# Starting a fused attention and MoE kernel on half of the first batch: first batch split by tokens, loads reordered

## The chip, the cores and the metric

One core of one Trainium2 chip. The metric is the device time of one execution in microseconds (us), given as the median of the runs of a kernel. In the profile PE is TensorE, PEld its weight loads, DVE is VectorE, ACT is ScalarE, POOL is GpSimd and SP is SyncE. L412 is line 412 of the kernel's file. The change adds lines, so a line of the new kernel has another number for the same work: L412 becomes L568 (first product), L430 becomes L586 (second product), L335 and L341 become L496 (last multiply of the attention of batch 0), and L371 becomes L527. Experiments shift the numbers by one or two again.

## The reference

```python
# q, k, v: (8, 8, 576, 64) f32;  w_in: (512, 2048);  w_out: (2048, 512)
scores = q @ k^T / 8
mask_local   = (0 <= i - j < 32)                     # heads 0 to 3
mask_strided = (j <= i) and (j % 32 == i % 32)       # heads 4 to 7
attn = softmax(where(mask, scores, -1e9)) @ v
x = attn.transpose(0, 2, 1, 3).reshape(4608, 512)
h = x @ w_in
out = relu(h)**2 @ w_out                             # (4608, 512) f32
```

## The kernel before

The kernel turns each batch's attention into columns of `xt`, x transposed, in bf16: four tiles of 128 rows, one for each pair of heads. The MoE part runs over chunks of 512 tokens. The **first product** of a chunk has 16 column blocks of four matmuls each, followed by ReLU (ScalarE) and a square (VectorE) into `g`; the **second product** multiplies g with w_out. Chunk 0 needs batch 0 alone, and a large part of the time before 50 us is spent on getting there. The order of instructions on each engine is the order of the program. These are the parts that the change touches:

```python
def first_steps():          # batch 0: a, b, c, d are its four pairs of heads
    t, n, o = T_, ..., ...  # t transposes q or k, S_ scores and exp, n sums and 1/sum, o product with v
    a, b, c, d = first_order                       # (0, 2, 3, 1)
    ...
    order = [(t(a, "q"), 0), (t(a, "k"), 2), (S_(a), 4), (t(b, "q"), 1), (t(b, "k"), 1), (S_(b), 0),
             (t(c, "q"), 0), (t(c, "k"), 0), (n(a), 0), (S_(c), 0), (n(b), 0),
             (t(d, "q"), 0), (t(d, "k"), 0), (o(a), 0), (S_(d), 0), (due(c), 0), (o(b), 0),
             (due(d), 0), (n(c), 0), (o(c), 0), (lambda: part((a, b), (0,)), 0), (n(d), 0), (o(d), 0),
             (lambda: part((a, b), (1, 2)), 0), (lambda: part((c,)), 0), (lambda: part((d,)), 0)]
    return order            # the numbers are spare matmuls that keep the clock up

gates = {1: w_in_b[0:1, 0, 1024:1025], 2: w_out_b[0:1, 8, 0:1]}

def loads(b):               # batch b; gate: a one-element GpSimd copy into the staging tile,
    u = 4 * b               # which must wait for the weights and so holds the load back
    for i in range(2):
        load_qk_local(u + i, nc.sync, gate=gates.get(b) if i == 0 else None)
    ... # v loads on the sync queue
    w_out(0)                # (batch 1 only) quarter of w_out, requested and cast by GpSimd
    load_qk_str(u + 2)
    cast_qk_local(u, pool2) # pool2: GpSimd casts
    w_out(1)
    cast_qk_local(u + 1, pool2)
    load_qk_str(u + 3)
    w_out(2)
    cast_v_local(u)
    cast_v_local(u + 1)
    w_out(3)
    ...

load_qk_local(0, nc.sync); load_qk_local(1, nc.sync)
load_qk_str(2)
make_identity(nc, ident)
load_qk_str(3)
...                         # memsets and masks
load_v_first()
cast_qk_local(1, pool2)
for i in range(4):
    load_w_in(i)
first = first_steps()
...
loads(1)
```

From batch 2 on the local part of the attention goes back through the same stream of requests: the sync queue carries, in program order, the loads of each batch, the transposes of strided q and k by DMA, and the transposes of the result (`xt<-x_l`), which free the tile `x_l` for the next batch.

The softmax here doesn't subtract the row's maximum and nothing guards it: scores larger than these inputs give would overflow.

## Time and profile before

| kernel before | value |
|---|---|
| time, median of 2 runs | 322.76 us (322.57 to 322.96) |
| profiled span | 319.6 us |
| first transposes of batch 0 | 4.95 us |
| first block of the first product begins | 21.07 us |
| last `xt` write of batch 0 ends | 24.4 us |
| second product of chunk 0 begins | 37.29 us |

The prediction below shows the stretches, the chain and the waits of this kernel. From the timeline of VectorE, then of GpSimd (start, length, engine, line, operation, tiles, idle time before and what ended it):

```profile
23.62 0.82 DVE L341 TENSOR_TENSOR xt<-pt,g_sb 128x288 bf16<-128x288 f32 x2 [0.89 <-ACT g_sb L317]
```

```profile
23.31 0.18 POOL L111 CAST q_st<-w_in_b 1x1 f32<-1x1 bf16 x1 [8.94 <-DMA w_in_b<-in_moe_w_in_dram]
...
48.27 0.18 POOL L111 CAST q_st<-w_out_b 1x1 f32<-1x1 bf16 x1 [0.38 <-DMA w_out_b<-in_moe_w_out_dram]
```

The first is the end of batch 0's attention. The other two are the gates of batch 1 and batch 2, the moments from which their loads may flow.

### The profile page before, as it was taken

The numbers are of one execution on the slowest core, as the hardware profiler recorded it, in microseconds if no ns is written. First come the engines' busy times: TensorE is split into PE (matmuls) and PEld (weight loads), VectorE is DVE, ScalarE is ACT, GpSimd is POOL, SyncE is SP. The second block draws the span as 40 slices with busy tenths as digits, with TensorE's granted clock in tenths as the row PEclk, the third lists the DMA queues.
The fourth block names the chain that finished last, engine by engine and source line by source line (L and its number), as shares of the span: only waits on it lengthen the run. The fifth ranks groups of instructions, "written<-read, shape, count | busy, mean of one in ns | idle before, by whom it ended". The sixth has DMA issues, their size and how long they took to land.

```text
span 319.6 us, 6138 instructions
## 1 busy us (share of the span) xinstructions
PE 300.0 (94%) x2322; PEld 149.5 (47%) x2364; DVE 170.7 (53%) x414; ACT 163.7 (51%) x337; POOL 87.8 (27%) x114
## 2 busy tenths in 40 slices
PE   7789978898999989999999999999999999999995
PEld 3454545444555444444444444444444444444442
DVE  6476463677956975676585557555555222222200
ACT  4576644477655755554554455545543443434311
POOL 8605472473930713271182015000000000000000
PEclk9859999999999999999999999999999999999999
DMA  7999999999999999999797677000411110000021
GB/s 182 172 205 227 221 155 251 186 328 208 198 162 210 197 212 182 212 242 188 183 211 167 145 159 133 35 33 33 53 51 36 55 42 36 33 33 35 35 96 66
DMA packets 87220, 44.79 MB, mean 140 GB/s; under 512 B 71768, under 2 KB 80376, under 8 KB 87000
## 3 DMA queue, kind: packets, MB, share of 16 engines
q1 hardware_dynamic: 77448, 34.81, 53.3%
q0 software_dynamic: 9744, 9.60, 18.9%
q8 instruction: 18, 0.29, 0.4%
q14 instruction: 10, 0.08, 0.1%
HBM read 36.89 MB, written 12.98 MB: 156 GB/s over the span
## 4 chain that ended last, share of the span: by engine, by line
PE 78%; DMA 9%; DVE 6%; ACT 3%; issue 2%; POOL 1%; SPq 0%; ACTq 0%; POOLq 0%
PE ph L412 33%; PE py L430 26%; PE ph L430 10%; PE pt L359 3%; PE pt L277 3%; DMA w_out_b<-in_moe_w_out_dram 3%; DMA q_st<-in_q_dram 3%; DMA kT_s<-in_k_dram 3%; DVE xt L396 1%; PE pt L388 1%; DVE e L288 1%; PE pt L233 1%; DVE g_sb L419 1%; ACT r L418 1%; ACT e L282 1%
## 5 line engine op out<-in xcount | busy, mean ns | idle before, releaser
L412 PE MATMUL ph<-xt,w_in_b 128*128 128x512 bf16 x557 | 143.3, 380 | 3.3 <-DVE xt L396 1.9
L418 ACT ACTIVATE r<-ph 128x512 bf16<-128x512 f32 x143 | 85.3, 597 | 99.5 <-PE ph L412 96.2
L419 DVE TENSOR_TENSOR g_sb<-r 128x512 bf16<-128x512 bf16 x144 | 71.2, 496 | 102.4 <-ACT r L418 101.9
L430 PE MATMUL py<-w_out_b,g_sb 128*128 128x512 bf16 x383 | 100.2, 379 | 1.3 <-issue 0.5
L430 PEld LDWEIGHTS <-g_sb 128*128 128x128 bf16 x576 | 52.9, 98 | 60.8 <-issue 4.3
L412 PEld LDWEIGHTS <-w_in_b 128*128 128x128 bf16 x576 | 51.7, 98 | 54.5 <-issue 1.3
L282 ACT ACTIVATE e<-pt 128x288 bf16<-128x288 f32 (+1 forms) x128 | 48.8, 406 | 17.0 <-PE pt L277 16.9
L430 PE MATMUL ph<-w_out_b,g_sb 128*128 128x512 bf16 x166 | 40.7, 379 | 1.9 <-DMA w_out_b<-in_moe_w_out_dram 1.2
L181 POOL CAST vl<-vl_st 128x768 bf16<-128x768 f32 x14 | 12.4, 886 | 60.2 <-DMA vl_st<-in_v_dram 58.1
L359 PEld LDWEIGHTS <-e 128*128 128x128 bf16 (+1 forms) x392 | 21.0, 97 | 15.6 <-DVE e L288 0.5
L371 DVE TENSOR_TENSOR x_s<-pt,rinv 72x384 bf16<-72x384 f32 (+1 forms) x42 | 21.4, 509 | 1.4
L288 DVE TENSOR_TENSOR e<-e,mask_str 72x576 bf16<-72x576 bf16 x32 | 18.0, 563 | 5.9 <-ACT e L282 5.6
L122 POOL CAST q_l<-q_st 96x768 bf16<-96x768 f32 x15 | 13.0, 865 | 21.9 <-DMA q_st<-in_q_dram 19.4
L288 DVE TENSOR_TENSOR e<-e,mask_loc 128x576 bf16<-128x576 bf16 x32 | 16.7, 523 | 1.7 <-ACT e L282 1.7
L122 POOL CAST k_l<-k_st 96x768 bf16<-96x768 f32 x15 | 13.3, 885 | 13.9 <-DMA k_st<-in_k_dram 13.8
L370 DVE RECIPROCAL rinv<-pt 96x6 f32<-96x6 f32 (+2 forms) x70 | 12.9, 184 | 7.8 <-PE pt L359 7.8
L434 ACT COPY y<-py 128x512 f32<-128x512 f32 x25 | 14.7, 587 | 4.0 <-PE py L430 4.0
L371 DVE TENSOR_TENSOR x_l<-pt,rinv 96x384 bf16<-96x384 f32 x28 | 15.5, 553 | 1.8 <-DMA xt<-x_l 0.9
L434 ACT COPY y<-ph 128x512 f32<-128x512 f32 x11 | 6.4, 586 | 19.4 <-PE ph L430 19.4
L197 POOL CAST vs<-v_st 72x1024 bf16<-72x1024 f32 x14 | 15.4, 1126 | 1.6 <-DMA v_st<-in_v_dram 1.3
L359 PE MATMUL pt<-vs,e 72*128 72x65 bf16 x224 | 13.7, 193 | 0.1
L182 POOL CAST vl<-vl_st 32x640 bf16<-32x640 f32 x14 | 11.9, 850 | 0.9
(77 smaller groups left out, 154.2 us busy)
## 6 DMA issues: line engine op xcount, KB each, us to landing
out_dram<-y SPq DMA_DIRECT2D x36, 256.0 KB, 2.0
vl_st<-in_v_dram SPq DMA_DIRECT2D x28, 144.0 KB, 4.0
v_st<-in_v_dram SPq DMA_DIRECT2D x14, 288.0 KB
q_st<-in_q_dram SPq DMA_DIRECT2D x8, 288.0 KB, 7.1
k_st<-in_k_dram SPq DMA_DIRECT2D x8, 288.0 KB, 7.9
q_st<-in_q_dram SPq DMA_DIRECT2D x16, 144.0 KB, 3.8
k_st<-in_k_dram SPq DMA_DIRECT2D x16, 144.0 KB, 5.9
w_in_b<-in_moe_w_in_dram POOLq DMA_DIRECT2D x4, 512.0 KB, 9.4
```

What stands on the lines that cost most here:

```text
L122: copy(t.rearrange("p j h d -> p h j d"), s[name + "f"].rearrange("p h (j d) -> p h j d", j=6))
L197: (copy or nc.gpsimd.tensor_copy)(t[:, :, 0:D], s["vf"].rearrange("p h (j d) -> p (h j) d", d=D))
L282: nc.scalar.activation(e[0:kn, lo:lo + S // 2], banks[row][half][0:kn, 0:S // 2], AF.Exp, scale=scale)
L288: nc.vector.tensor_tensor(x, x, m.to_broadcast([kn, n, w]), op=ALU.mult)
L359: nc.tensor.matmul(po[:, n - n0, :], e[0:kn, pos(n):pos(n) + 128], rhs[0:kn, src(n), 0:D + 1], start=True, stop=True)
L370: nc.vector.reciprocal(rinv[0:w, 0:m], po[0:w, 0:m, D:D + 1])
L371: nc.vector.tensor_tensor(x, po[0:w, 0:m, 0:D], rinv[0:w, 0:m].to_broadcast([w, m, D]), op=ALU.mult)
L412: nc.tensor.matmul(ph, w_in_b[:, kk, 128 * ff:128 * (ff + 1)], xt[kk][:, 512 * c:512 * (c + 1)], start=(kk == order[0]), stop=(kk == order ...
L418: nc.scalar.activation(r, ph, AF.Relu)
L419: later(1, lambda: nc.vector.tensor_tensor(g[:, ff, :], r, r, op=ALU.mult))
L430: nc.tensor.matmul(py, g[:, ff, 128 * j:128 * (j + 1)], w_out_b[:, ff, :], start=(ff == 0), stop=(ff == 15))
L434: nc.scalar.copy(y, py)
```

## The change

Its intent: tokens 0 to 287 of batch 0 need only keys 0 to 287, so half of q, k and v is loaded first, its attention is finished, and 12 blocks of the first product run on tokens 0 to 255 while the second half's attention is worked out between them. The second half's rows are held back by a gate, so that they don't compete with the first half's. GpSimd issues the first two quarters of w_in ahead of everything that waits on it (at 3.89 and 6.68 us; the third, at 13.12, stands behind a cast). Local v of batch 0 comes by the sync queue now and is cast by GpSimd; before, GpSimd's own transfers cast it on the way. In batch 1's loads, two quarters of w_out come ahead of the rest, and the casts of v behind all four. The core of the diff, with cuts marked by "...":

```diff
+    def load_local_half(hf):
+        ...
+            if hf == 1 and name == "q":          # the hold-back
+                nc.gpsimd.tensor_copy(t[0:1, 0, 0:1], vl0[32:33, 0, 0, 0:1])
+        ...
     def first_steps():
-        ... four pairs of heads, each step of one next to steps of the others
+        ... first half: transposes, scores, masks, sums, products; then
+        m = lambda ff, kks=range(4), pool=None: mm1(0, ff, kks, pool, 0, CH)      # CH = 256 tokens
+        ...                                       # blocks 0 to 2
+        cast_half(1, "k", V)
+        cast_half(1, "q", A)
+        cast_v_local_half(1, G)                   # GpSimd, ahead of loads(1)
+        m(3)
+        half_T("l", 1, "k", V)
+        half_T("l", 1, "q", V)
+        half_T("s", 1, "q", V)
+        m(4)
+        ex = half_S("l", 1)
+        ex[0]()
+        m(5)
+        ...                                       # one link of the second half, one block, and so on
+        m(11)
+        half_mask("s", 1, 1)
+        half_N("s", 1)
+        half_O("s", 1)
 ...
         w_out(0)
+        w_out(1)
         load_qk_str(u + 2)
         cast_qk_local(u, pool2)
-        w_out(1)
-        cast_qk_local(u + 1, pool2)
         load_qk_str(u + 3)
+        cast_qk_local(u + 1, pool2)
         w_out(2)
+        w_out(3)
         cast_v_local(u)
         cast_v_local(u + 1)
-        w_out(3)
 ...
-    load_v_first()
-    cast_qk_local(1, pool2)
-    for i in range(4):
-        load_w_in(i)
+    load_w_in(0)
+    ...
+    load_v_str_a()
+    load_w_in(1)
+    cast_v_local_half(0, nc.gpsimd.tensor_copy)
+    load_local_half(1)
+    load_v_local_half(1)
+    load_str_half(1, "q")
+    load_str_half(1, "k")
+    load_w_in(2)
+    first_steps()                                 # w_in 3 is in it
     for t in vl_sts:                              # memsets, now behind first_steps
         nc.vector.memset(t[0:32], 0.0)
 ...
-    for ff in range(16):
-        add(0, 1, ff) if ff >= NP else add(0, 0, ff)
+    for ff in range(12):
+        add(0, 0, ff, ps_h)                       # tokens 256 to 511 of blocks 0 to 11
+    for ff in range(12, 16):
+        add(0, 0, ff)
+        add(0, 0, ff, ps_h)
```

## The prediction

> **What bounds the kernel now.** I began with the page's busy shares and chain. TensorE is busy 300.0 of 319.6 us, so at most 19.6 us of waiting is to be had, plus what is done at a low clock. I then cut the span into stretches, to see where those 19.6 us lie, and read the wait list and the chain in order of time for the first 64 us.
>
> The stretches of the kernel before (columns: stretch, its length, busy PE, PEld, DVE, ACT, POOL, granted clock, DMA share, GB/s):
>
> ```profile
> 2.26:10.90 8.64, 6.28 (x46) 2.47 (x43) 4.60 (x28) 2.79 (x6) 7.43 (x13) 1.00 1.30 221
> 10.90:37.40 26.50, 24.60 (x228) 13.44 (x231) 17.00 (x38) 18.75 (x41) 11.18 (x16) 0.81 1.23 207
> 37.40:48.30 10.90, 8.40 (x105) 4.66 (x104) 6.75 (x14) 5.16 (x13) 7.18 (x10) 1.00 1.08 176
> 48.30:100.00 51.70, 47.53 (x511) 26.21 (x521) 34.35 (x81) 31.18 (x69) 25.82 (x31) 1.00 1.13 219
> 100.00:302.00 202.00, 198.38 (x1374) 96.22 (x1400) 106.55 (x250) 101.58 (x204) 35.14 (x42) 1.00 0.57 113
> ```
>
> The reader is to see that 202 us of the span have only 3.6 us of PE idle: nothing is to be won there. The change acts before 48 us, where DMA is full (share above 1) and PE idles about 2.4, 1.9 and 2.5 us in the first three rows. The 8.64 us of the first row are mostly warm-up matmuls, so useful work is scarcer than busy time says.
>
> From the chain in order of time (start, length, what):
>
> ```profile
> 2.26 8.60 DMA kT_s<-in_k_dram
> ...
> 24.43 9.16 DMA q_st<-in_q_dram
> ...
> 37.43 10.79 DMA w_out_b<-in_moe_w_out_dram
> 48.22 0.04 issue
> 48.26 1.02 PE ph L430 x4
> ```
>
> Three transfers carry the start: strided k of batch 0, q of batch 1, and the third quarter of w_out, which is what the second product waits for. The wait list of the first 60 us gives GpSimd's part:
>
> ```profile
> POOL q_st L111 <- DMA w_in_b<-in_moe_w_in_dram: 8.9, 1, 8.9
> PE ph L430 <- DMA w_out_b<-in_moe_w_out_dram: 1.2, 1, 1.2
> ```
>
> GpSimd is parked 8.9 us, until w_in's third quarter lands at 23.3 us. This gate holds batch 1's loads back. PE pays 1.2 us directly for w_out. In the timeline, the first matmul of the first product (L412) starts at 21.07, the unbroken run at 25.55, and it ends at 37.19.
>
> **What the Trainium skill says.** "TensorE: Matmul & The Clock Gate", Part 1, says that PE drops to half clock after a quiet window of about 3.4 us and returns after a busy one. The trace agrees: in 2 us stretches the clock is 0.72, then 0.50 four times, then 0.72 in 12 to 24 us, after PE was busy only 2.0 of 8 to 12 us. The same page, "Single matmul latency", gives (398 + N)/2.4 ns; for N = 512 that is 379 ns, and L412's row shows 380. "DMA: Bandwidth & Descriptors", Rules for kernel authors, says that transfers from different issuers share the same 16 engines, so more queues bring no bandwidth; the trace's DMA share stays above 1 whichever queue issues.
>
> **The change part by part.**
>
> *1. Token halves.* Tokens 0 to 287 need only keys 0 to 287, so their attention can finish on half of q, k and v. Then 12 of the 16 column blocks of the first product run on tokens 0 to 255 inside the second half's attention. By 25.55 the kernel before had done 3 full blocks (0.865 us each, four matmuls at 0.216); the new one should have done 12 half blocks, worth 6. That is 3 x 0.865 = 2.6 us ahead, if the second half ends no later than the old batch 0 did (about 24.4, from the last xt write at 23.62 plus 0.82).
>
> *2. When the second half can end.* Bytes read from HBM: q, k, v of batch 0 are 3 x 1.18 = 3.54 MB; a quarter of w_in or w_out is 1.05 MB. Before, 3.54 + 0.09 + 3 x 1.05 = 6.78 MB had come by 23.31, from 2.26 on: 322 GB/s. After, the order on the queues is first half (local q and k 0.59, strided q and k 0.59, v local with overlaps 0.36, v strided 0.295: 1.83 MB), w_in 0 and 1, second half (0.59 + 0.59 + 0.39 = 1.57), w_in 2: 6.55 MB, so 20.3 us at that rate, 22.6 us on the clock. All of strided v (0.59 MB) follows, 1.8 us more: 24.4, perhaps 25 once batch 1's loads compete. Then the last product with v, the multiply (two of about 0.41 to 0.6 us) and xt: **about 26.5 us**. So the second half ends 2 us later than the old batch 0, and most of the 2.6 us is spent.
>
> *3. The rest of the first product.* Left are 12 second halves and four blocks in two halves: 20 groups of four 128x256 matmuls. Pure issue is 4 x 0.109 = 0.44 us, 8.7 us in all: an end at 35.2, which is 2.0 us early. But every group takes one of two PSUM banks. Its last matmul is issued at 0.33 and ends 0.27 later (398 + 256 over 2.4), at 0.60; the ReLU then takes 0.38 (597 ns for 512 columns and 406 for 288 give 0.85 ns per column); so two groups take about 1.03 us, 0.52 each, and 20 take 10.3. Also the memsets that stood in the first 5 us now follow the second half on VectorE: 1.5 + about 1.5 us from the old timeline; with four r buffers that costs PE about 0.6 us. The end lies between 35.2 and 37.5 us; I take 36.5, so 0.7 us early.
>
> *4. w_out.* Before its third quarter lands, 0.59 + 1.05 (last w_in) + 3.54 (batch 1) + 3.15 = 8.33 MB must follow the 6.55: 14.88 MB against 14.52 before, because of v's overlap and of the first half of strided v read twice. At 322 GB/s that is 46.2 us after 2.26: **48.5 us, against 48.22**. Issuing two quarters first moves bytes about within the same queue, but takes none out ahead of the third. What helps is that GpSimd no longer has casts between the requests: before, the second stretch ran at 7.74 MB in 24.9 us, 311 GB/s. I allow 1 us either way.
>
> *5. Extra instructions.* Strided transposes double in number (16 of 36 columns per tensor and half), exponentials fall from 16 to 14, ReLUs of block 0 rise from 16 to 32: 16 x (2 x 0.38 - 0.60) = 2.6 us of ScalarE. Most lies beside data waits.
>
> Sum: part 1 gains 2.6, parts 2 and 3 give back about 1.9, and w_out's third quarter caps the remainder. The cap is the step that ends last: 48.26 stays near 47 to 48.5. Later idle changes little. I choose a gain of 1.5 us, a little above what the cap alone gives, as w_out's first two quarters come earlier and the 2.5 us of idle in 37 to 48 can shrink: 322.76 - 1.5 = 321.3 us.
>
> **The rivals.**
>
> *A. The clock.* If the fill-in matmuls keep PE above the gate's threshold, the half-clock stretch (10 us before, about 5 us of full-clock work lost) goes, and the second half's attention runs faster. For: 128-row matmuls replace gaps. Against: that stretch waits for data in the new order, so a faster PE only waits longer. If it counts, 318 us or less. The reverse, a low clock reaching into the 20 groups, costs 2 to 4 us: 324 to 326.
>
> *B. The weights come earlier.* If DMA was short of requests while GpSimd sat 8.9 us in its gate, dense issuing raises the rate; 345 GB/s would put the third quarter at 45.4 us and save close to 3 us: 319 to 320. Against: the share is above 1 throughout.
>
> *C. A new wait in program order.* PE is in order, and block 8 needs w_in's third quarter. If that is late, the second half's sums and products queue behind it, and everything slips by 1 to 3 us: 323 to 325.
>
> *D. The gain is hidden anyway*, by w_out: 322 to 323. This is nearest to my sum.
>
> **How the range follows.** D and my sum give 320.5 to 323; B reaches to 319, A to 318; C and the low clock reach to 325. The range 318.3 to 324.2 leaves about a tenth on each side. Faster by 2% means below about 316.4: it needs A and B together, 0.04. Slower by 2%, above 329.2, needs a low clock and C together: 0.03.
>
> **What would show each step.** Part 1: first 256-column matmul of the first product at 13 to 16 us, against 21.07. Part 2: last xt write of batch 0 at about 26.5. Part 3: start-to-start of groups near 0.52 us rather than 0.44, the last at about 36.5, and a VectorE run of memsets after 26 us. Part 4: the product with w_out's third quarter starts at 47 to 48.5, with a wait on that DMA ahead of it. From 100 us on, everything is shifted by a constant. I am wrong if the second half ends before 24 us, if the third quarter lands before 46, or if the clock shows 0.5 beyond 26 us.

## More of the kernel before

From the chain of waits in order of time, and from the groups of instructions (busy us, mean ns, idle before and its main releaser):

```profile
63.19 1.25 PE ph L412 x5
```

```profile
L371 DVE TENSOR_TENSOR x_l<-pt,rinv 96x384 bf16<-96x384 f32 x28 | 15.5, 553 | 1.8 <-DMA xt<-x_l 0.9
```

The chain line is the first long piece of chunk 1's first product; I use its start as the mark of how late the start of the kernel has come. The group line says that `x_l` is hardly ever waited for: 0.9 us in the whole execution.

## The result, and the profile after

The changed kernel is **slower**: 334.87 us median of 2 runs (334.35 to 335.38), with the right output; the ratio to the kernel before is 1.0376 (95% interval 1.0335 to 1.0417). A ratio here is the mean time of one kernel's fast runs over that of the other's of the same rounds, so not quite the ratio of the medians that are quoted. Executions over 1.5% slower than the fastest of the same kernel are left out of the means. The profiled span is 332.7 us against 319.6: 13.1 us more.

The stretches of the kernel after, cut at its own landmarks (columns as in the prediction):

```profile
2.26:20.40 18.14, 13.65 (x178) 7.56 (x177) 6.58 (x16) 7.49 (x18) 9.98 (x20) 0.81 1.16 206
20.40:35.20 14.80, 10.66 (x179) 7.53 (x180) 8.78 (x25) 8.60 (x24) 4.59 (x7) 0.89 0.87 159
35.20:46.90 11.70, 11.43 (x83) 8.46 (x83) 8.11 (x37) 7.35 (x20) 5.75 (x8) 0.85 1.20 222
...
101.30:112.00 10.70, 7.22 (x62) 3.44 (x60) 3.07 (x9) 3.09 (x9) 2.47 (x3) 0.84 1.19 193
112.00:314.00 202.00, 198.38 (x1388) 96.33 (x1414) 105.75 (x251) 101.17 (x203) 35.77 (x42) 1.00 0.57 110
```

The last row, 202 us long, has PE busy 198.38 us, the same as the row of 100 to 302 us that the prediction shows of before. So nearly all of the loss (about 12.8 of the 13.1 us, by the same piece of the chain in both) lies ahead of 112 us, and it lies in two places. The first is the stretch from 20.4 to 35.2 us, where DMA falls to a share of 0.87 and PE idles 4.1 us; the second is a hole of 3.5 us of PE idle in the row of 101.3 to 112. Between 105 and 110 us PE works for 2.42 of 5 us, where the kernel before worked for all 5.00.

**The first place.** The chain of the kernel after:

```profile
3.67 7.06 DMA vl_st<-in_v_dram
...
13.29 7.07 DMA k_st<-in_k_dram
...
34.01 0.07 DVE xt L496
...
35.23 4.13 PE ph L568 x21
39.37 0.04 issue
39.40 1.03 PE ph L568 x8
```

Read it from the top. The first half's v lands at 10.7 us; that opens the gate of the second half, whose k is requested at 13.29 and lands at 20.36. From there to 35.2 the chain is no DMA at all: it goes from engine to engine in pieces of under 1 us. VectorE's timeline of the same kernel has the ends of that stretch:

```profile
17.55 1.18 DVE L496 TENSOR_TENSOR xt<-pt,g_sb 128x288 bf16<-128x288 f32 x2 [0.49 <-ACT g_sb L466]
20.45 0.56 DVE L349 CAST k_l<-k_st 96x768 bf16<-96x768 f32 x1 [1.72 <-DMA k_st<-in_k_dram]
...
34.01 1.17 DVE L496 TENSOR_TENSOR xt<-pt,g_sb 128x288 bf16<-128x288 f32 x2 [1.88 <-ACT g_sb L466]
35.28 1.51 DVE L797 MEMSET vl_st<- 32x768 f32 x2
```

The first half is done at 18.7 us; the second takes from 20.45 to 35.2, 14.8 us, and batch 0 is complete 10.8 us later than before (24.4). What follows to the start of the second product takes 11.7 us (35.23 to 46.95) against 12.9 us before (24.4 to 37.29), so 1.1 us of the 10.8 come back, and the second product begins 9.7 us later.

**The second place.** GpSimd's timeline, and its longest wait in the first 64 us:

```profile
28.59 0.82 POOL L335 CAST g_sb<-vl_st 128x768 bf16<-128x768 f32 x1 [12.53 <-DMA vl_st<-in_v_dram]
29.36 0.18 POOL L119 CAST q_st<-w_in_b 1x1 f32<-1x1 bf16 x1
...
57.42 0.18 POOL L119 CAST q_st<-w_out_b 1x1 f32<-1x1 bf16 x1
```

```profile
POOL g_sb L335 <- DMA vl_st<-in_v_dram: 16.0, 2, 12.5
```

GpSimd comes to the cast of the second half's v and waits 12.5 us for v. Batch 1's gate stands behind it in program order and opens at 29.36 (23.31 before), batch 2's at 57.42 (48.27 before). No request of batch 1 can be out in the meantime, and from 28 to 32 us the DMA share is 0.31. The stream stays late to the end: the transposes that free `x_l`.

```profile
101.28 5.60 DMA xt<-x_l
```

```profile
L527 DVE TENSOR_TENSOR x_l<-pt,rinv 96x384 bf16<-96x384 f32 x28 | 15.5, 553 | 5.9 <-DMA xt<-x_l 4.8
```

They start at 101.28 us (88.95 before), and the wait for them is 4.8 us instead of 0.9. They are 12.3 us late, while PE's own work is late by less, as the mark in the chain shows:

```profile
71.74 1.24 PE ph L568 x5
```

**A sum of two shifts** follows, which every later run is held against: the mark moved from 63.19 to 71.74, P = 8.55 us, and the wait for `x_l` grew by 3.9; together 12.5 of the 13.1 us.

### The profile page after: what moved, and what is told of

Read it like the earlier page. It is cut to its first block, busy times and chain, and to the rows that moved or that the text cites. A ratio compares the mean times of both kernels' runs of the same rounds, so it can differ in the third digit from the quotient of the medians.

```text
span 332.7 us, 6551 instructions
## 1 busy us (share of the span) xinstructions
PE 306.9 (92%) x2495; PEld 157.9 (47%) x2537; DVE 170.4 (51%) x427; ACT 165.8 (50%) x352; POOL 87.6 (26%) x118
## 4 chain that ended last, share of the span: by engine, by line
PE 82%; DMA 6%; DVE 5%; ACT 2%; issue 2%; SPq 1%; POOL 0%; DVEq 0%; ACTq 0%; POOLq 0%
PE ph L568 36%; PE py L586 26%; PE ph L586 10%; PE pt L515 3%; PE pt L285 3%; DMA k_st<-in_k_dram 2%; DMA vl_st<-in_v_dram 2%; DMA xt<-x_l 2%; PE pt L544 1%; PE pt L241 1%; DVE xt L552 1%; DVE x_s L527 1%; SPq L314 1%; DVE g_sb L575 1%; ACT r L574 1%
## 5 line engine op out<-in xcount | busy, mean ns | idle before, releaser
L568 PE MATMUL ph<-xt,w_in_b 128*128 128x512 bf16 (+1 forms) x623 | 148.2, 362 | 3.6 <-DVE xt L552 1.9
L574 ACT ACTIVATE r<-ph 128x512 bf16<-128x512 f32 (+1 forms) x159 | 88.2, 555 | 104.9 <-PE ph L568 101.2
L575 DVE TENSOR_TENSOR g_sb<-r 128x512 bf16<-128x512 bf16 (+1 forms) x160 | 73.0, 461 | 104.7 <-ACT r L574 103.1
L568 PEld LDWEIGHTS <-w_in_b 128*128 128x128 bf16 x640 | 58.3, 99 | 52.9 <-issue 3.8
L290 ACT ACTIVATE e<-pt 128x288 bf16<-128x288 f32 (+1 forms) x112 | 43.2, 406 | 11.4 <-PE pt L285 11.2
L586 PE MATMUL ph<-w_out_b,g_sb 128*128 128x512 bf16 x167 | 42.3, 387 | 0.5
L130 POOL CAST q_l<-q_st 96x768 bf16<-96x768 f32 x14 | 11.9, 851 | 24.2 <-DMA q_st<-in_q_dram 23.3
L526 DVE RECIPROCAL rinv<-pt 96x6 f32<-96x6 f32 (+2 forms) x70 | 12.9, 184 | 9.0 <-PE pt L515 9.0
L130 POOL CAST k_l<-k_st 96x768 bf16<-96x768 f32 x14 | 12.3, 879 | 18.2 <-DMA k_st<-in_k_dram 15.5
L296 DVE TENSOR_TENSOR e<-e,mask_loc 128x576 bf16<-128x576 bf16 x28 | 15.2, 543 | 1.5 <-ACT e L290 1.5
L296 DVE TENSOR_TENSOR e<-e,mask_str 72x576 bf16<-72x576 bf16 x28 | 13.4, 478 | 2.3 <-ACT e L290 2.2
L515 PE MATMUL pt<-vs,e 72*128 72x65 bf16 x224 | 13.4, 193 | 0.0
```

The source lines that it names most:

```text
L130: copy(t.rearrange("p j h d -> p h j d"), s[name + "f"].rearrange("p h (j d) -> p h j d", j=6))
L290: nc.scalar.activation(e[0:kn, lo:lo + S // 2], banks[row][half][0:kn, 0:S // 2], AF.Exp, scale=scale)
L296: nc.vector.tensor_tensor(x, x, m.to_broadcast([kn, n, w]), op=ALU.mult)
L515: nc.tensor.matmul(po[:, n - n0, :], e[0:kn, pos(n):pos(n) + 128], rhs[0:kn, src(n), 0:D + 1], start=True, stop=True)
L526: nc.vector.reciprocal(rinv[0:w, 0:m], po[0:w, 0:m, D:D + 1])
L568: nc.tensor.matmul(ph, w_in_b[:, kk, 128 * ff:128 * (ff + 1)], xt[kk][:, 512 * c + lo:512 * c + hi], start=(kk == 0), stop=(kk == 3))
```

## The experiments

Two theories for the first place:

- *Chain*: the second half's attention is a string of small dependent steps that runs after the first half's, instead of beside it, so that batch 0 needs two such strings one after the other.
- *Data* (rival): its rows come too late, because of the hold-back or because of v.

A third suspect beside these was the clock of TensorE. For the second place the suspect was the order on GpSimd. All kernels that ran gave the right output. No experiment beat the kernel before.

### e1_nohold and e2_v1dma: earlier data

```diff
# e1_nohold: no hold-back
-            if hf == 1 and name == "q":
-                nc.gpsimd.tensor_copy(t[0:1, 0, 0:1], vl0[32:33, 0, 0, 0:1])
# e2_v1dma: v of the second half by GpSimd's own casting transfers, requested behind strided k; no cast left on GpSimd
-    load_v_local_half(1)
+    for i in range(NL // 2):
+        nc.gpsimd.dma_start(out=vl0[:, NL // 2 + i], in_=v[0, 0:4]...)
-        cast_v_local_half(1, G)
```

> The changed kernel without the one-element copy that holds the second half's local q, k and v back until GpSimd has cast the first half's v. Theory V (the second half's v, on the sync queue, lands last at 28.6 us and GpSimd's cast of it stands ahead of everything): v lands near 15 us instead, GpSimd passes the cast by 17 us, batch 1's loads start when the third quarter of w_in lands (about 25 instead of 29.5 us), the last xt write of batch 0 moves from 35.2 to about 30 us; time 327 to 330 us. Rival H (k of the second half, landing at 20.4 us, is what costs): the same gain, with the k cast near 12 us. Rival C (half clock, two banks and memsets in the 20 half groups cost most): 333 us or more.

> The changed kernel with the second half's local v loaded by GpSimd's casting transfers (as the kernel before did), ahead of the third quarter of w_in; the GpSimd cast of it is gone, the hold-back stays. Theory V: the 12.5 us wait of GpSimd is gone, the gate of batch 1 passes when the third quarter of w_in lands (24 to 26 us), the last xt write comes at about 31 us; time 327 to 331 us. Rival H (k at 20.4 us is what costs): 333 to 335 us. Rival C: 333 us or more.

Measured: e1_nohold 330.66 us, ratio 1.0255 (1.0164 to 1.0346); e2_v1dma 331.69, ratio 1.0271 (1.0188 to 1.0354). In e1_nohold the second half's k was cast at 17.80 us instead of 20.45, and yet the last `xt` write ended at 35.3, as in the kernel after (35.2); in e2_v1dma, where v needed no cast, it ended at 35.35. So **earlier data of the second half did not bring its end forward**. For k the trace shows the reason: its rows were cast 2.65 us earlier in e1_nohold, but its transposes stand in TensorE's program behind the first half and its blocks 0 to 2, and began at 20.63 us against 21.06 in the kernel after. The second string thus starts only when the first half and its three blocks are through, and from VectorE's copy of the transposed k to the last `xt` write it takes about 13.4 us in all three kernels. A low clock hid a part of the gain: in this execution the four spare matmuls ahead of the blocks took 1.89 us, against 1.04 in the kernel after, so the earlier k may be worth about 1 us at full pace (an estimate from these two and the 0.4 us that did come). The gain has another source. In e1_nohold v lands earlier, and GpSimd's order moves up:

```profile
25.16 0.83 POOL L333 CAST g_sb<-vl_st 128x768 bf16<-128x768 f32 x1 [9.75 <-DMA vl_st<-in_v_dram]
25.93 0.27 POOL L119 CAST q_st<-w_in_b 1x1 f32<-1x1 bf16 x1
```

The gates open at 25.93 and 53.67 (e2_v1dma: 24.09 and 53.54), the mark is at 72.35 (72.10), no earlier than in the kernel after, and the wait for `x_l` is gone in both. The ratio falls by 0.0105 to 0.0121, 3.4 to 3.9 us: the size of that wait. The intervals of these ratios just overlap that of the kernel after (1.0335 to 1.0417); the reading rests on the traces, in which the gates come earlier, the wait vanishes and the span falls by 4.4 us or more. This shows the second place to be GpSimd's order, with the first place unchanged.

### e3_gatefirst: the gate ahead of the cast

```diff
+        loads1_head()               # batch 1: gate, local q and k, one v, w_out 0 and 1, strided q and k
         cast_v_local_half(1, G)
```

> The changed kernel with batch 1's gate, its q, k and first v on the sync queue, the first half of w_out and the first strided unit issued ahead of GpSimd's cast of the second half's v. If batch 1's late loads cost the time: loads start near 25 us, DMA idles no more in 28 to 32 us, and the time falls to 328 to 331 us. If the late end of batch 0's second half costs it (PE has nothing to do until xt is complete): last xt write still at 35 us or later, time 333 to 336 us.

Measured: 333.51 us, ratio 1.0340 (1.0256 to 1.0425). The gates came at 23.59 and 49.82, nearly as early as in the kernel before, and the wait for `x_l` vanished, as expected; but the start got worse. The last `xt` write ended at 38.3 and the second product began at 50.12, so the mark came at 75.27. Part of it can be read off: GpSimd's casts now lie beside VectorE's steps of the second half. VectorE, then GpSimd, in this kernel:

```profile
29.34 0.29 DVE L575 TENSOR_TENSOR g_sb<-r 128x256 bf16<-128x256 bf16 x1 [0.87 <-ACT r L574]
...
32.10 0.84 DVE L575 TENSOR_TENSOR g_sb<-r 128x256 bf16<-128x256 bf16 x1 [1.90 <-ACT r L574]
```

```profile
31.98 0.82 POOL L130 CAST q_l<-q_st 96x768 bf16<-96x768 f32 x1 [1.04 <-DMA q_st<-in_q_dram]
```

The same multiply takes 0.29 us alone and 0.84 beside a cast that runs until 32.80. "SBUF — State Buffer" in the Trainium skill, section "SBUF: two separate sides", says that GpSimd and VectorE share a pair of ports, and that whoever takes it first has it for its whole instruction, against a VectorE operation with two SBUF inputs among others. The trace agrees: the multiply reads r twice, and ends 0.14 us after the cast. Two such cases cost 1.1 us. The rest of the 3.1 us by which the `xt` write came later was there before the gate opened: VectorE's copy of the transposed k began at 23.67 us instead of 21.73. TensorE was at a clock of 0.50 until about 20 us in this execution, against about 15 in the kernel after, while GpSimd's order ahead of the gate is the same in both; so this part is not shown to be the gate's doing.

### e4_wofirst: the new order of w_out on the kernel before

```diff
         w_out(0)
+        w_out(1)
         load_qk_str(u + 2)
         ...                         # as in the change, on the kernel before
```

> The kernel before with only the order of w_out changed: first two quarters one after the other ahead of batch 1's strided q and k. If this part does nothing (the third quarter still lands near 48 us): 322 to 324 us. If it delays batch 1's strided unit: 325 us or more, with PE waiting for its transposes at 43 us.

Measured: 327.02 us (324.16 to 329.07), ratio 1.0097 (0.9989 to 1.0206): unclear. In the profiled run the mark was at 64.35, 1.2 us late, and `x_l` waited 3.9 us. The stream was only 2.0 us late at its transposes (90.93), but these took 8.1 us to the next write instead of the 6.3 of before. So this part may cost a per cent by itself; the spread of its runs does not allow a firmer word.

### e5_alone, e6_tail, e7_all: nothing between the links, nothing behind them

```diff
# e5_alone: the blocks 4 to 11 of the first product moved behind the second half's last link
-        m(4)
-        tick()
         ...
+        for ff in range(4, 12):
+            m(ff)
+            tick()
# e6_tail: late memsets moved to the start or cut to what is read; every third half block in a third PSUM bank
-        nc.vector.memset(t[0:32], 0.0)
+        nc.vector.memset(t.rearrange("p (h t) d -> p h t d", h=2)[0:32, :, 0, :], 0.0)
+            p3 = ps_y if len(groups) % 3 == 2 else None
# e7_all: e1_nohold, e5_alone and e6_tail together
```

> The changed kernel with half blocks 4 to 11 of the first product moved behind the second half's attention, so that nothing stands between the links of its chain on any engine. First three runs showed that neither k, nor v, nor GpSimd's gate moves the last xt write from 35 us. Theory I (the interleaved blocks, in order on TensorE, ScalarE and VectorE, stretch the chain): last xt write at 30 to 31 us, the 28 groups then take about 15 us, second product at about 45 to 46 instead of 46.95 us, time 332 to 335 us. Rival L (the chain of one half is latency-bound by itself, some 14 us, whatever stands between): last xt still at 33 to 35 us, second product at 49 to 51, time 337 to 340 us.

> The changed kernel with the late memsets taken out of VectorE's way (most back at the start, the staging one cut to the two blocks that need zeros) and with the third PSUM bank in turn with the two for the 20 half groups. If banks and memsets cost what I worked out (1.6 and 0.6 us): groups 0.44 us apart at full clock, second product at about 45 instead of 46.95 us, time 332 to 333.5 us. If only the half clock sets the pace there: second product at 46 us or later, time 334 to 335.

> Three edits at once: no hold-back of the second half, half blocks 4 to 11 behind its attention, memsets and third bank as in e6_tail. If their gains add (4 from the hold, 0 to 2 from the order, 2 from the tail): 326 to 329 us. If the start is bound by something that none of them touches (the two chains in series): 328 us or more, last xt write of batch 0 no earlier than 29 us.

Measured: e5_alone 333.86 us, ratio 1.0349 (1.0271 to 1.0428). The second half, with TensorE to itself, ran from 20.25 to 33.8 us: 13.5 us instead of 14.8. Counted from VectorE's copy of the transposed k the string takes 11.2 us against 13.45 in the kernel after (10.3 in e10_warm, at full clock). So the blocks in between cost 2 to 3 us, and the larger part of the length is the string's own. Stretches of e5_alone:

```profile
24.00:28.00 4.00, 2.88 (x64) 2.25 (x63) 2.00 (x5) 2.77 (x9) 0.00 (x0) 0.50 0.83 138
28.00:32.00 4.00, 2.04 (x52) 1.89 (x52) 1.19 (x3) 2.06 (x6) 3.77 (x7) 0.50 0.44 94
```

No engine but GpSimd is busy for much over half of the second row: that is a chain, in which each waits for another. And with the blocks gone TensorE falls to half clock, which gives back part of what the cleared path won; the eight moved blocks then come on top, and the second product began at 50.72.

e6_tail: 334.74 us, ratio 1.0403 (1.0288 to 1.0518). The half blocks came 0.44 us apart instead of 0.53, and the second product began at 44.70 instead of 46.95. The mark moved up to 69.21, but `x_l` waited 6.1 us, so nothing was left of it at the end. (0.7 of the 2.3 us by which the second product came earlier lies in the second half itself, which ended at 34.5.) It shows that the two places are tied: a start that comes earlier runs into the late stream.

e7_all: 331.18 us, ratio 1.0274 (1.0187 to 1.0362). k was cast at 19.07, the last `xt` write ended at 32.2, the mark came at 70.97, and the wait was 2.0 us.

### e8_winlater: w_in behind the first half's v

```diff
-    load_w_in(0)
     ...
     load_v_str_a()
+    load_w_in(0)
     load_w_in(1)
```

> The changed kernel with w_in's first quarter requested behind the first half's v instead of ahead of it. If the early weight transfer delays the first half's k (cast at 7.69 us, against 5.17 before): k cast at 5.5 to 6.5 us and all of the first half 1 to 2 us earlier, time 332.5 to 334 us. If k is late for another reason (four smaller transfers, strided q and k beside them): cast still after 7 us, time 334 to 336 us.

Measured: 335.20 us, ratio 1.0393 (1.0299 to 1.0486). A miss: k of the first half was cast at 7.23 us against 7.69 in the kernel after and 5.17 before. w_in's first quarter is not what delays the first half's rows. Why the first transposes come at 8.30 us instead of 4.95, with half the bytes asked for, stays open in the main. In the trace k takes two requests instead of one, and the last goes out at 2.2 us instead of 1.27, which is 0.9 of the 2.5 us by which k's cast is later; why its rows then take 5.4 us instead of 3.9 to land is not shown.

### e9_pipe: the second half's chain pulled into the first half's

```diff
# without the hold-back, with the edits of e6_tail; strided q and k of the second half requested ahead of w_in 1
         half_N("l", 0, True)
+        cast_half(1, "k", V)
+        cast_half(1, "q", A)
         half_O("l", 0)
-        half_N("s", 0)
-        half_O("s", 0)
-        ...                         # blocks 0 to 3
+        half_T("l", 1, "k", V)
+        half_T("l", 1, "q", A)
+        half_N("s", 0)
+        ex = half_S("l", 1)         # and so on: one link of each half in turn,
+        ...                         # blocks 0 to 3 near the end, 4 to 11 behind it
```

> Hold-back gone, memsets and third bank as in e6_tail, strided q and k of the second half requested ahead of w_in's second quarter, and the second half's transposes and scores set between the links of the first half's chain, so that the two chains overlap. The runs so far fit a sum of two shifts: P, how late the first block of chunk 1 starts on TensorE (63.2 us in the kernel before, 71.7 in the changed one), and what it then waits for a slot of x_l (0.9 us before, 4.8 after), which the load stream sets. If two chains in series cause P: last xt write of batch 0 at 27 to 30 us, P 3 to 5 instead of 8.5 us. The load stream is only about 4 us earlier than in the changed kernel, so the wait returns: 327 to 330 us. If not: last xt write at 32 us or later, time 331 us or more.

Measured: 328.95 us, ratio 1.0164 (1.0092 to 1.0235). VectorE:

```profile
15.08 0.56 DVE L347 CAST k_l<-k_st 96x768 bf16<-96x768 f32 x1 [1.79 <-DMA k_st<-in_k_dram]
...
27.73 1.90 DVE L494 TENSOR_TENSOR xt<-pt,g_sb 128x288 bf16<-128x288 f32 x4
```

The second half ends at 29.6 us, 5.6 earlier than in the kernel after and 2.6 earlier than in e7_all, although the clock is 0.50 from 10 to 24 us. The mark comes at 66.04. This is the most direct evidence for *chain*: the same arithmetic on the same halves, with the two strings side by side. The 5.6 us are the work of all its edits together; against e7_all, which shares the others, overlapping brings 2.6, and as strided q and k of the second half were also requested earlier in e9_pipe, not even these are separated from that. The wait for `x_l` is 4.4 us again, as the batches' gates (25.18 and 50.97) did not move up with the start.

### e10_warm: the separate chain at full clock

```diff
# e7_all, with 22 spare matmuls on a zeroed tile between the second half's links
+        warm(4)
         ...
+        warm(8)
```

> e7_all with 22 spare matmuls on a zeroed tile between the links of the second half's chain, to keep the clock up (0.50 in 24 to 32 us there). If the half clock costs: clock 1.00 from 20 to 36 us, last xt write 1 to 2 us earlier than 32.2, the first 8 blocks at full clock, P 2 to 3 us below e7's 7.8; time 329 to 331, held by the load stream. If it doesn't: P as in e7 or later by the spare work, 331 to 333 us.

Measured: 327.15 us, ratio 1.0149 (1.0094 to 1.0205). The clock stayed at 1.00 from 16 us on, and the second half ran from 17.75 to 30.6 us, 12.9 us long, against 13.2 in e7_all. The last `xt` write came 1.6 us earlier (1.3 of it from a k cast that came earlier), the second product 2.0 us earlier (43.08), and the mark 3.1 us earlier (67.89). The ratio fell by 0.0125, 4 us, of which 2.0 are the wait for `x_l`, which vanished. The 1.3 us of the earlier k cast are not the doing of matmuls that stand behind it. The chain itself got 0.3 us shorter, and 0.4 us were won between the last `xt` write and the second product: the 40 half blocks there took 5.31 us instead of 6.58, and the spare matmuls ahead of them took most of this back. The other 1.1 us of the mark came after the second product had begun, where the clock reads 1.00 in both kernels. So the low clock of e7_all is worth at most about 1.6 us in this comparison, and 0.7 net of the spare work.

### e11_both and e12_pipegate: the gate first, once more

```diff
# e11_both: e1_nohold, e3_gatefirst and e6_tail together
# e12_pipegate: e9_pipe with loads1_head() ahead of the v cast, as in e3_gatefirst
```

> Hold-back gone, batch 1's gate and first loads ahead of the cast of v, memsets and third bank mended; order of the blocks as in the change. By the sum of two shifts: P about 6 (as e6_tail), load stream as early as in e3 (gate of batch 2 at 50 us), so no wait for x_l: 326 to 329 us. If P does not come down with less DMA contention, 330 us or more.

> e9_pipe with batch 1's gate and first loads ahead of the cast of the second half's v: both shifts attacked. If both causes are the right ones: P 3 to 5, no wait for x_l, 324 to 327 us. If the split of batch 0 is worth anything over the kernel before, it would show here, below 322; I expect not.

Measured: e11_both 331.39 us, ratio 1.0247 (1.0184 to 1.0309); the mark at 73.07 and no wait for `x_l`. e12_pipegate 330.68 us, ratio 1.0237 (1.0180 to 1.0294), no gain over e9_pipe, its profiled run slow (365.75 us), so no cause is read from it. In e11_both the second half ended 2.4 us later than in e1_nohold (37.7 against 35.3), but 2.0 of these were there at the copy of the transposed k (23.89 against 21.92), before the gate opened at 24.74. That an earlier gate pays with a later start is therefore not shown by e3_gatefirst and e11_both.

### e13_pipewarm and e14b_pipewarmv: what is left once the chains overlap

```diff
# e13_pipewarm: e9_pipe, with 14 spare matmuls between its links
# e14b_pipewarmv: e13_pipewarm, v of the second half as in e2_v1dma, but requested ahead of w_in 2
```

> The ninth experiment (second half's transposes and scores pulled into the first half's chain, no hold-back, late memsets out of the way, third bank) with 14 spare matmuls on a zeroed tile added where TensorE waits in it, so that the clock does not fall to 0.5. There the second half's last xt write ended at 29.6 us and the second product began at 40.97, at clock 0.50 from 12 to 24 us. Theory (series chain plus low clock make the late start, and a second limit, the stream of loads on the sync queue, sets the end when it is later): xt ends at 27 to 28, second product starts at 38.5 to 39.5, the fifth-block landmark of the chain at 64 to 65, but x_l still waits 4 to 6 us for xt<-x_l, so that the total hardly moves: 327 to 329.5 us. Rival (only the start on TensorE counts, waits later are absorbed): the total falls by what the start gains, to about 326 or less. Rival (clock is not what costs): xt stays at 29 or later.

> The kernel of e13_pipewarm, but the second half's v is cast by its own GpSimd transfers, requested ahead of w_in's third quarter, so that no GpSimd cast stands between w_in and batch 1's gate; one memset of a staging tile moves to the start. In e13_pipewarm the clock stayed at 1.00 from 8 us on and still the second half's last xt write ended at 29.55 us; there its scores and exponentials were done by 23.4 and the product with v waited for the v cast, which GpSimd began at 25.16 after 9.53 us of waiting for v. New theory for the start: once the chains overlap, the arrival of v is what binds, as the prediction had assumed for the kernel of the change. It expects: v there by 22 to 23, last xt write ended at 26.5 to 27.5, second product begins at 39 to 40 (the issue of 28 groups of 0.44 us after it). Rival: the chain itself still binds and xt ends at 29 to 29.6 again. For the stream: theory (the loads of batch 1 onwards are a second limit that starts at batch 1's gate) expects the gate at 24 instead of 25.93, batch 2's gate at 50 to 52 instead of 53.77, the wait of x_l under 2.5 us instead of 4.1, and a total of 324 to 326.5 us; rival (order of w_out's quarters or bytes alone) keeps the wait at 4 us and the total within 1 us of the 328.2 of e13_pipewarm.

Measured: e13_pipewarm 328.18 us (323.99 to 329.66), ratio 1.0116 (1.0042 to 1.0191). Of e13_pipewarm, from the timelines of TensorE, GpSimd and VectorE together:

```profile
22.23 1.04 PE L602 MATMUL py<-wz 128*128 128x512 bf16 x4
...
25.16 0.82 POOL L334 CAST g_sb<-vl_st 128x768 bf16<-128x768 f32 x1 [9.53 <-DMA vl_st<-in_v_dram]
...
27.65 1.90 DVE L495 TENSOR_TENSOR xt<-pt,g_sb 128x288 bf16<-128x288 f32 x4
```

The four spare matmuls take 1.04 us, so TensorE runs at its full pace there, and still the second half ends at 29.55 us: from about 17 us on the clock is not what costs in this kernel, and there the rival of the expectation was right. (Before that the record misleads: the column reads 1.00 from 8 us on, but two spare matmuls at 11.51 took 1.03 us, where two at full pace take about half of that.) Now the last link, the product with v, begins at 26.29, just after the cast of v that GpSimd could begin at 25.16 ended at 25.98. But it also stands in TensorE's program right behind two half blocks, and the chain of waits runs through these and not through v:

```profile
25.33 1.03 PE ph L567 x8
26.36 0.38 PE pt L477 x12
```

So v and the blocks were through within 0.4 us of each other, and which of them binds is not shown. Arrival of v is close to what the prediction had put down for it (24.4 to 25 us). The mark is at 64.97, only 1.8 us late, and `x_l` waits 4.1 us: mostly the second place by itself. The figures of the trace are those of one execution of 328.83 us, the slowest fast one of its kernel (324.0 to 328.8).

e14b_pipewarmv: 328.72 us, ratio 1.0180 (1.0120 to 1.0241). The gates (24.39 and 51.83) and the wait for `x_l` (2.3 us) came as the theory of the stream had expected, but the start was a miss: the last `xt` write ended at 33.4 instead of 27, and the mark came at 69.55. v's rows, asked for earlier on GpSimd's queue, delayed the others (k was cast at 16.65 instead of 15.30), and TensorE stayed slow for longer, so that the expectation about v stays undecided. A stretch and a row of TensorE's timeline of e14b_pipewarmv:

```profile
20.00:24.00 4.00, 4.00 (x78) 2.38 (x73) 2.66 (x6) 1.32 (x4) 0.00 (x0) 1.00 1.28 201
```

```profile
22.15 1.89 PE L602 MATMUL py<-wz 128*128 128x512 bf16 x4
```

The same four spare matmuls take 1.89 us, half pace, in a stretch where the column of the granted clock says 1.00. So in this kernel the clock is probably part of the loss after all (no run takes it from there alone), and the duration of a known matmul is the better witness of it.

### All runs against the sum of two shifts

P is how much later than 63.19 us the mark came, W the wait for `x_l` less 0.9 us, and D the profiled span less 319.6 us; all in us.

| kernel | second half ends | P | W | P + W | D | ratio |
|---|---|---|---|---|---|---|
| after | 35.2 | 8.6 | 3.9 | 12.5 | 13.1 | 1.0376 |
| e1_nohold | 35.3 | 9.2 | -0.9 | 8.3 | 8.6 | 1.0255 |
| e2_v1dma | 35.4 | 8.9 | -0.9 | 8.0 | 8.7 | 1.0271 |
| e3_gatefirst | 38.3 | 12.1 | -0.9 | 11.2 | 14.8 | 1.0340 |
| e4_wofirst | - | 1.2 | 3.0 | 4.2 | 3.7 | 1.0097 |
| e5_alone | 33.8 | 12.0 | -0.9 | 11.1 | 11.8 | 1.0349 |
| e6_tail | 34.5 | 6.0 | 5.2 | 11.2 | 12.0 | 1.0403 |
| e7_all | 32.2 | 7.8 | 1.1 | 8.9 | 9.8 | 1.0274 |
| e8_winlater | 35.0 | 8.2 | 4.3 | 12.5 | 15.0 | 1.0393 |
| e9_pipe | 29.6 | 2.9 | 3.5 | 6.4 | 7.2 | 1.0164 |
| e10_warm | 30.6 | 4.7 | -0.9 | 3.8 | 4.7 | 1.0149 |
| e11_both | 37.7 | 9.9 | -0.9 | 9.0 | 10.5 | 1.0247 |
| e13_pipewarm | 29.6 | 1.8 | 3.2 | 5.0 | 7.5 | 1.0116 |
| e14b_pipewarmv | 33.4 | 6.4 | 1.4 | 7.8 | 7.2 | 1.0180 |

P + W comes within 1 us of D in ten of the fourteen. In e3_gatefirst, e8_winlater, e11_both and e13_pipewarm, D is 1.5 to 3.6 us larger; what makes up the rest there was not traced. Each row is one profiled execution, and fast executions of one kernel differ by up to 4.8 us (e13_pipewarm), so small differences between rows prove little.

## Why the prediction was wrong

The predicted time was 321.3 us, with 0.93 on a change within 2%; measured were 334.87 us and 3.8% slower. By its steps:

1. **Token halves: the blocks ran where they were put, but late.** The first half block began at 17.79 us, not at 13 to 16. The first half itself came late (first transposes at 8.30), and e8_winlater did not find out why.
2. **When the second half can end: this is the step that failed.** The prediction took the arrival of the last data (24.4, perhaps 25 us) and added one product and one multiply: about 26.5. Measured were 35.2. The byte count behind it was good only for a kernel without the hold-back: v was there at 25.16 in e1_nohold, but at 28.6 in the kernel after, about 4 us later than counted. That was not what set the end. What it left out is the string of steps between k and the last write: 14.8 us from 20.45 in the kernel after, 12.9 at best in e10_warm. The prediction saw those steps as lying beside data waits because in the kernel before they did: there four pairs of heads overlapped, and the whole of batch 0's attention took 19.5 us from its first transposes. Halving by tokens halves the work of a step, but hardly the length of the string: in the kernel before the whole batch needed 13.5 us from its last chain transfer (10.9) to its last write (24.4). It also puts two strings in a row: 11.0 us for the first (7.69 to 18.7) and 14.8 for the second. Earlier data left the end where it was (e1_nohold, e2_v1dma); overlapping the strings took 5.6 us off together with the edits of e7_all, and 2.6 us against e7_all (e9_pipe). Only then did v's arrival come near to binding (e13_pipewarm; it is not separated from two half blocks there), and even then the end came 4.4 us after it, not 2, as all four multiplies come at once (1.90 us).
3. **The rest of the first product: mechanism right, size a little off.** Pairs of half blocks came 1.07 us apart against the 1.03 worked out from two PSUM banks, and the memsets stood where they were expected (35.28 to 38.3). The stretch took 11.7 us instead of about 10, as it began at half clock: the first 21 matmuls took 4.13 us, where the later pace of 8 in about 1.07 us gives 2.8, so about 1.3 us were lost to it (an estimate from these two figures). The clock at 0.50 beyond 26 us was named as a sign of a wrong prediction, and it was there, from 32 to 38 us. e6_tail brought the pitch to the 0.44 us of pure issue.
4. **w_out as a cap: fell away.** With the second product 9.7 us later, TensorE no longer waits for w_out in the list of waits. The cap was a fact of the kernel before, not of the new one.
5. **"Later idle changes little": wrong, and worth 3.9 us.** (The shift from 100 us on was constant indeed: the same pieces of the chain come 12.8 us later at 114.69 and at 314.90 us.) The prediction counted the bytes of batch 1 but not where its gate stands in GpSimd's program. The removal of casts from between the requests was seen as a gain for w_out; that the one cast left stands ahead of the gate, and waits 12.5 us for v, was not seen. Removing the wait gave 3.4 to 3.9 us back (e1_nohold, e2_v1dma).

The first three terms put the second product at 36.5 us, and it came at 46.95: that is the larger error, and step 5 is the smaller one. Of the rivals, C had the right form, a new wait in program order that lets everything slip, but it named w_in's third quarter, for which nothing waited, and gave it 1 to 3 us. A, the clock, was real but smaller than the 2 to 4 us given for a low clock (about 1.3 us by the estimate of step 3, at most 1.6 in e10_warm), and not the main term. The prediction's reading of the clock gate, "the trace agrees", doesn't hold in full either: between 8 and 12 us TensorE's longest pause in the kernel before was 1.05 us, not 3.4, and the clock stayed at 0.50 from 14 to 22 us while TensorE was busy 6.9 of the 8 us. What stays open: why the first half's rows come 2.5 us later than whole rows did before (0.9 us of it is the later request); how much the order of w_out costs by itself (e4_wofirst, unclear); whether v or the half blocks bind in e13_pipewarm; how long TensorE stays at half pace at the start, which differed between the profiles (to about 15 us in the kernel after, 17 in e13_pipewarm, 28 in e14b_pipewarmv); and 1.5 to 3.6 us in four of the experiments.

## What to carry to other kernels

Before splitting a startup into two halves, measure how long its string of dependent steps is from first data to last write, with the data there: a half does half the work but, in this case, nearly the same string, and two strings in a row lose more than early data gain, unless one is threaded into the other. On an engine that also issues transfers or opens gates, look at what stands in program order ahead of each request: one cast that waits for its data holds back every later batch, and that shows tens of microseconds later as a wait of another engine. And when the predicted path is shortened, ask which stream now ends last: a start that came 2.3 us earlier (e6_tail) gave nothing, because the stream of loads was as late as ever.

## What the Trainium skill lacked or had wrong

- "TensorE: Matmul & The Clock Gate", the part "Seeing it yourself", warns that the records of the clock gate are not to be trusted fully. The runs give it a number: in e14b_pipewarmv four matmuls of 512 columns took 1.89 us from 22.15 us on, against 1.04 in e13_pipewarm, while the granted clock reads 1.00 in both. In e13_pipewarm itself two such matmuls took 1.03 us at 11.51 us, with the column at 1.00 as well. Here it was the duration of a known matmul that showed it.
- "DMA: Bandwidth & Descriptors" calls the making of descriptors for GpSimd's transfers "small, variable". Here each request of a quarter of w_in or of w_out occupies GpSimd for 0.75 to 0.78 us, and one of strided q or k for 0.67 to 0.70 us, in program order with its casts.
- No page was found to have the point that cost 3.4 to 3.9 us here: that a gate and a cast that waits, both on GpSimd, put a whole stream of loads behind the cast's data (12.53 us of waiting at 28.59 us).
